# Linear attention and a gated MLP: loading q in 1-KB rows, with the transposed layout and the order of work that follow from it

## The chip, the cores and the metric

The kernel runs on one core of a Trainium2 chip. The metric is the device time of one execution in microseconds (us); medians of several runs are quoted. TensorE does the matmuls, ScalarE and VectorE (ACT and DVE in the profile) copy and combine, GpSimd (POOL) casts and scales, and SyncE (SP) issues most loads. In this kernel matmuls write to PSUM; the tiles that they read lie in SBUF. A run is called slow when it lies over 1.5% above the fastest of its kernel; only fast runs are compared, and a difference counts as faster or slower from 2% on. A profile's span is about 2 us shorter than the time of the same run (156.3 us beside 158.19 us for the profiled run of before).

## The reference

Causal attention with a decay `lam` per head, without softmax, in blocks of 64 tokens with a carried state, feeds a gated MLP whose gate mixes tokens:

```python
# q, k, v: 4 x 8 heads x 768 tokens x 64; lam: 8 heads
for b in range(nb):                                   # blocks of 64 tokens
    intra = einsum('bhic,bhjc->bhij', qb, kb) * Dmask # lam ** (i - j), causal
    out   = intra @ vb + (qb * lam_pow) @ kv_state
    kv_state = lam_block * kv_state + (kb * rev_pow)^T @ vb
x = out as (batch, seq, 512)
h = relu(x @ w_in)                                    # 1024 wide: u, v
v_n = (v - mean(v)) / sqrt(var(v) + 1e-6)
y = (u * (w_spatial @ v_n + b_spatial)) @ w_out
```

## The kernel before

Work is cut into 12 tiles of 256 tokens with all 8 heads, three tiles to a batch. Partition p of a tile holds tokens 2p and 2p + 1 (`m` below), so a packet of a load is 2 tokens x 64 x 4 bytes = 512 bytes. k and q are scaled and cast, transposed on TensorE (tiles 0 to 7), and copied out of PSUM: kT by ScalarE, qT by VectorE, which multiplies the decays in on the way. Scores, a mask and two groups of products build `pat` in PSUM. ScalarE copies it to `xT`, and in doing so puts the tokens, which lie as (m, p), back into the order 2p + m. All projections read `xT`.

```python
def load_x(x, src, n):                    # q, k and v alike: 512-byte rows
    # [...]
    nc.sync.dma_start(out=t.rearrange("p h m d -> p h (m d)"),
        in_=src[b, :, r * T2:(r + 1) * T2].rearrange("h (p m) d -> p h (m d)", m=2))
# [...]
def copy_kT(n):
    nc.scalar.activation(out=transposed(n, "kT"), in_=st[n]["pt"][:, 0], func=AF.Copy)

def copy_qT(n):                           # every tensor bf16 and dense
    nc.vector.tensor_tensor(out=transposed(n, "qT"), in0=st[n]["pt"][:, 1],
        in1=lq[:, n % NR].rearrange("p m g x -> p (m g) x"), op=ALU.mult)
# [...]
def copy_x(n):                            # written at a step of 2 elements
    # [...]
    nc.scalar.activation(
        out=xT[b][:, r].rearrange("p c g (d m) -> p (c g) m d", m=2),
        in_=st[n]["po"].rearrange("p c g (m d) -> p (c g) m d", m=2), func=AF.Copy)
# [...]
order = """
    q:0 q:1 k:0 k:1 v:0 q:2 [...] ld:0 cq:0 q:4 lq:0 cq:1 lq:1 ck:0 k:4
    lq:2 ck:1 k:5 T:0 qT:0 T:1 kT:0 qT:1 cq:2 kT:1 A:0:0 A:0:1 [...]
```

The words of `order` are the program: `q:0` loads q of tile 0, `ck`/`cq` scale or cast, `T` transposes, `A` are the scores, `a` the mask, `xT` the copy above, `pv`/`pu` the projections, `pvs` the token mixing, `po` the output.

## Time and profile before

| | before |
|---|---|
| median time (3 runs) | 158.95 us |
| span of the profiled run | 156.3 us |
| TensorE busy | 132.8 us (85%) |
| VectorE / ScalarE / GpSimd busy | 94.0 / 78.0 / 77.7 us |
| first transposes on TensorE | 11.80 us |
| first v projection | 27.22 us |

Busy time on TensorE alone fills 85% of the span, and most of the rest is the wait at the start. So what a change does to TensorE's holes decides. The prediction below shows the slices, the start of the timeline and the groups. The timeline: start us, duration us, engine, line, operation, out<-in, and in brackets the idle time before and what ended it; PEld is TensorE loading weights.

```profile
25.70 2.48 ACT L308 ACTIVATE xT<-pat 128x1024 bf16<-128x1024 f32 x2 [0.70 <-PE pat L299]
27.22 0.13 PEld L325 LDWEIGHTS <-xT 128*128 128x128 bf16 x2 [0.17 <-ACT xT L308]
27.22 1.99 PE L325 MATMUL pv<-win_sb,xT 128*128 128x512 bf16 x8
```

A copy takes 1.3 us (1322 ns on average), and the projection starts at 27.22 without any hole on TensorE: other matmuls lie between, just long enough to cover the copy. How little room is left shows in the bracket of the weight load: it was already waiting, 0.17 us, for the copy.

### The profile page before, as it was taken

How to read it: one execution, taken by the hardware profiler on the slowest of the kernel's cores; microseconds unless marked ns; L12 is line 12 of the kernel's file. 1: busy time of each engine (PE TensorE's matmuls, PEld its weight loads, DVE VectorE, ACT ScalarE, POOL GpSimd, SP SyncE). 2: the span in 40 equal slices, each digit the busy share in tenths (PEclk: the TensorE clock that was granted, in tenths of full speed). 3: DMA queues.
4: the chain of work that ended last, by engine and by line, in shares of the span. 5: the costliest groups of instructions: out<-in, count | busy, mean ns of one | idle time of the engine just before them, and what ended most of it. 6: DMA issues, size and time to landing. Idle time of an engine off the chain costs nothing.

```text
span 156.3 us, 4534 instructions
## 1 busy us (share of the span) xinstructions
PE 132.8 (85%) x1992; PEld 88.7 (57%) x1992; DVE 94.0 (60%) x167; ACT 78.0 (50%) x103; POOL 77.7 (50%) x63
## 2 busy tenths in 40 slices
PE   0009469989989999989899999999999999999970
PEld 0008469646868667836665567665665557646440
DVE  1401975696967958656982874787395976424510
ACT  3896234564869423546555033658543376022360
POOL 4076966720359299799802059937220066470000
PEclk9999965999999999999999999999999999999996
DMA  2999999999998999994596995991890011006085
GB/s 43 305 291 290 290 247 295 246 261 212 260 271 260 269 277 204 296 292 124 143 294 115 229 244 125 180 268 31 259 256 33 0 72 66 0 0 268 10 319 208
DMA packets 51987, 30.70 MB, mean 196 GB/s; under 512 B 9472, under 2 KB 48896, under 8 KB 51968
## 3 DMA queue, kind: packets, MB, share of 16 engines
q1 hardware_dynamic: 49312, 27.53, 68.3%
q0 software_dynamic: 2368, 2.75, 10.5%
q8 instruction: 15, 0.25, 0.7%
q10 hardware_dynamic: 288, 0.14, 0.3%
q14 instruction: 4, 0.03, 0.1%
HBM read 24.78 MB, written 6.29 MB: 199 GB/s over the span
## 4 chain that ended last, share of the span: by engine, by line
PE 57%; DMA 16%; SPq 9%; ACT 8%; DVE 4%; POOL 3%; issue 1%; POOLq 0%; ACTq 0%
PE pvs L371 20%; PE po L409 12%; DMA k_in<-in_k_dram 11%; PE pv L325 9%; SPq L72 9%; PE pu L360 8%; DMA v_in<-in_v_dram 5%; ACT wt_sb L461 3%; PE pat L299 2%; ACT vh L330 2%; POOL kd L165 2%; PE pt L191 2%; PE pam L227 1%; ACT kT L202 1%; ACT uT L365 1%
## 5 line engine op out<-in xcount | busy, mean ns | idle before, releaser
L235 DVE TENSOR_TENSOR a<-pam,causal 128x1024 bf16<-128x1024 f32 x24 | 28.7, 1219 | 9.2 <-PE pam L227 9.1
L371 PE MATMUL pvs<-wt_sb,vn 128*128 128x384 bf16 x192 | 32.9, 326 | 0.3 <-ACT wt_sb L461 0.2
L397 POOL TENSOR_TENSOR gT<-h,uT 128x768 bf16<-128x768 f32 x12 | 19.6, 1644 | 21.6 <-PE po L409 16.1
L165 POOL TENSOR_TENSOR kd<-k_in,ldec 128x1024 bf16<-128x1024 f32 x12 | 23.3, 1944 | 12.0 <-DMA k_in<-in_k_dram 11.2
L371 PEld LDWEIGHTS <-vn 128*128 128x128 bf16 x192 | 18.4, 98 | 12.3 <-issue 0.2
L360 PE MATMUL pu<-xT,win_sb 128*128 128x256 bf16 x192 | 22.6, 273 | 0.0
L325 PE MATMUL pv<-win_sb,xT 128*128 128x512 bf16 x96 | 22.3, 380 | 0.0
L386 DVE TENSOR_TENSOR h<-pvs,bsp_bc 128x768 f32<-128x768 f32 (+1 forms) x17 | 15.3, 904 | 11.4 <-PE pvs L371 11.4
L431 ACT ACTIVATE o<-po 128x1024 f32<-128x1024 f32 x11 | 11.3, 1023 | 20.5 <-PE po L409 20.1
L337 DVE BATCH_NORM_STATS2 st<-vh 128x6 f32<-128x512 bf16 x24 | 16.1, 672 | 7.9 <-ACT vh L330 7.9
L178 POOL CAST vc<-v_in 128x1024 bf16<-128x1024 f32 x12 | 12.5, 1044 | 16.7 <-DMA v_in<-in_v_dram 16.7
L308 ACT ACTIVATE xT<-pat 128x1024 bf16<-128x1024 f32 x12 | 15.7, 1322 | 9.8 <-PE pat L299 9.8
L360 PEld LDWEIGHTS <-win_sb 128*128 128x128 bf16 x192 | 18.5, 98 | 3.5 <-issue 0.2
L191 PE MATMUL pt<-ident,kd 128*128 128x128 bf16 x64 | 5.8, 242 | 14.2 <-POOL kd L165 14.2
L330 ACT ACTIVATE vh<-pv 128x1024 bf16<-128x1024 f32 x12 | 12.3, 1023 | 10.0 <-PE pv L325 9.2
L409 PE MATMUL po<-wout_sb,gT 128*128 128x512 bf16 x72 | 16.7, 379 | 0.5 <-DVE s L263 0.5
L365 ACT ACTIVATE uT<-pu 128x1024 bf16<-128x1024 f32 x12 | 12.3, 1024 | 8.9 <-PE pu L360 8.9
L325 PEld LDWEIGHTS <-xT 128*128 128x128 bf16 x96 | 9.0, 98 | 10.2 <-issue 0.2
L202 ACT ACTIVATE kT<-pt 128x1024 bf16<-128x1024 bf16 x8 | 8.2, 1022 | 12.8 <-PE pt L191 10.1
L205 DVE TENSOR_TENSOR qT<-pt,lq 128x1024 bf16<-128x1024 bf16 x8 | 5.5, 691 | 14.4 <-PE pt L191 9.7
L352 DVE TENSOR_SCALAR vn<-vh,mv,rstd 128x512 bf16<-128x512 bf16 x24 | 13.3, 596 | 0.4
L191 PEld LDWEIGHTS <-kd 128*128 128x128 bf16 x64 | 4.6, 109 | 15.6 <-POOL kd L165 14.9
(58 smaller groups left out, 154.3 us busy)
## 6 DMA issues: line engine op xcount, KB each, us to landing
q_in<-in_q_dram SPq DMA_DIRECT2D x12, 512.0 KB, 7.5
k_in<-in_k_dram SPq DMA_DIRECT2D x12, 512.0 KB, 7.4
v_in<-in_v_dram SPq DMA_DIRECT2D x12, 512.0 KB, 7.7
out_dram<-o SPq DMA_DIRECT2D x11, 512.0 KB, 2.8
wsp_raw<-in_moe_w_spatial_dram POOLq DMA_DIRECT2D x1, 1152.0 KB, 13.4
win_sb<-in_moe_w_in_dram POOLq DMA_DIRECT2D x2, 512.0 KB, 9.2
...
```

Of the source, the lines that this page charges most:

```text
L72: nc.sync.dma_start(out=t.rearrange("p h m d -> p h (m d)"), in_=src[b, :, r * T2:(r + 1) * T2].rearrange("h (p m) d -> p h (m d)", m=2))
L165: eng.tensor_tensor(out=o, in0=st[n][x], in1=table[:, n % NR].rearrange("p m h -> p h m").unsqueeze(3) .broadcast_to((P, H, 2, D)), op=ALU ...
L235: nc.vector.tensor_tensor(out=s["a"][:, i].rearrange("p h g c x -> p (h g) c x"), in0=s["pam", i].rearrange("p h g c x -> p (h g) c x"), i ...
L308: nc.scalar.activation(out=xT[b][:, r].rearrange("p c g (d m) -> p (c g) m d", m=2), in_=st[n]["po"].rearrange("p c g (m d) -> p (c g) m d ...
L325: nc.tensor.matmul(out=p[:, j], lhsT=xT[b][:, r, j, c, :], rhs=win_sb[:, c, DH:DFF], start=(c == 0), stop=(c == NCH - 1))
L330: nc.scalar.activation(out=vh[:, 2 * r:2 * r + 2, :], in_=ps["v", b, r], func=AF.Relu)
L337: nc.vector.bn_stats(out=st6[:, t, :], in_=vh[:, t, :])
L360: nc.tensor.matmul(out=p[:, f], lhsT=win_sb[:, c, f * P:(f + 1) * P], rhs=xT[b][:, r, :, c, :], start=(c == 0), stop=(c == NCH - 1))
L371: nc.tensor.matmul(out=p[:, i, 0:HW_], lhsT=gm["vn", b][:, s, f * P:(f + 1) * P], rhs=wt_sb[:, s, i * HW_:(i + 1) * HW_], start=(s == 0), ...
L386: nc.vector.tensor_tensor(out=h[:, i], in0=ps["s", b, f][:, i, 0:HW_], in1=bsp_bc.rearrange("p (i x) -> p i x", i=2)[:, i], op=ALU.add)
L397: eng.tensor_tensor(out=gT[:, f, :].rearrange("p (i x) -> p i x", i=2)[:, i], in0=ps["h", b, f][:, i], in1=gm["uT", b][:, f, :].rearrange( ...
L409: nc.tensor.matmul(out=o, lhsT=gT[:, c, t * P:(t + 1) * P], rhs=wout_sb[:, c, f0:f0 + fn], start=(c == 0), stop=(c == NCH - 1))
```

## The change

The intent is cheaper loads of q. A row of q now holds 4 tokens (1 KB); to keep all 128 partitions filled, partition 2p + f holds tokens 4p to 4p + 3 of heads 4f to 4f + 3. Each load becomes two issues, one for each f. What follows from this layout is most of the diff: after the transposes the columns alternate between the two halves of the heads, so copy_qT reads them at a step of two; tokens now lie as (m, p) with m = 4, so copy_x writes at a step of four; the decays of q depend on the partition's parity and need a second small load of `lam`. The order of work was made anew for it.

```diff
+    def load_q(n):
+        b, r = divmod(n, NR)
+        t = st[n]["q"] = fin.tile([P, 4, 4, D], FP32, tag="q", name=f"q_in_{n}")
+        for f in range(2):
+            nc.sync.dma_start(
+                out=t[f::2].rearrange("p j m d -> p j (m d)"),
+                in_=q[b, 4 * f:4 * f + 4, r * T2:(r + 1) * T2].rearrange(
+                    "j (p m) d -> p j (m d)", m=4))
[...]
+    lam_f = const.tile([P, 4], FP32)
+    nc.scalar.dma_start(out=lam_f, in_=lam.rearrange("(f j) -> f j", f=2).unsqueeze(0)
+                        .to_broadcast((D, 2, 4)))
[... tables of positions and decays for the new layout ...]
     def copy_qT(n):
-        nc.vector.tensor_tensor(out=transposed(n, "qT"), in0=st[n]["pt"][:, 1],
-                                in1=lq[:, n % NR].rearrange("p m g x -> p (m g) x"), op=ALU.mult)
+        nc.vector.tensor_tensor(
+            out=transposed(n, "qT").rearrange("p g (f x) -> p g f x", f=2),
+            in0=st[n]["pt"][:, 1].rearrange("p g (x f) -> p g f x", f=2),
+            in1=lq[:, n % NR].rearrange("p m j f x -> p (m j) f x"), op=ALU.mult)
[...]
         nc.scalar.activation(
-            out=xT[b][:, r].rearrange("p c g (d m) -> p (c g) m d", m=2),
-            in_=st[n]["po"].rearrange("p c g (m d) -> p (c g) m d", m=2), func=AF.Copy)
+            out=xT[b][:, r].rearrange("p c g (d m) -> p (c g) m d", m=4),
+            in_=st[n]["po"].rearrange("p c g (m d) -> p (c g) m d", m=4), func=AF.Copy)
[... order: each engine's own words stay in the same order; between two engines the pair qT:1, kT:1 is turned round: ...]
-        lq:2 ck:1 k:5 T:0 qT:0 T:1 kT:0 qT:1 cq:2 kT:1 A:0:0 A:0:1 cv:0 wv v:4 q:5 a:0:0 K:0
+        lq:2 ck:1 k:5 T:0 qT:0 kT:0 T:1 kT:1 qT:1 cq:2 A:0:0 A:0:1 a:0:0 cv:0 wv v:4 q:5 a:0:1
```

More of the change, by code (lines that the diff above doesn't have):

```diff
@@ L44 @@
     NPE = 8
+    CKD = ()
+    CVA = ()
     T2 = 2 * P
@@ L73, in load_x @@
                           in_=src[b, :, r * T2:(r + 1) * T2].rearrange("h (p m) d -> p h (m d)", m=2))
+    def load_q(n):
[6 more added lines that the diff above has]
+                    "j (p m) d -> p j (m d)", m=4))
     lam_bc = const.tile([P, H], FP32)
     nc.scalar.dma_start(out=lam_bc, in_=lam.unsqueeze(0).to_broadcast((P, H)))
+    lam_f = const.tile([P, 4], FP32)
+    nc.scalar.dma_start(out=lam_f, in_=lam.rearrange("(f j) -> f j", f=2).unsqueeze(0)
+                        .to_broadcast((D, 2, 4)))
     kpos_i = const.tile([P, NR, 2], I32)
     nc.gpsimd.iota(kpos_i, pattern=[[-T2, NR], [-1, 2]], base=P - 1, channel_multiplier=-2)
-    qpos_i = const.tile([P, 2, P], I32)
-    nc.gpsimd.iota(qpos_i, pattern=[[1, 2], [2, P]], base=1 - P, channel_multiplier=0)
-    rel_i = const.tile([P, 2, 2, D], I32)
+    qpos_i = const.tile([P, 4, D], I32)
+    nc.gpsimd.iota(qpos_i, pattern=[[1, 4], [4, D]], base=1 - P, channel_multiplier=0)
+    rel_i = const.tile([P, 2, 4, 32], I32)
     for c in range(2):
-        nc.gpsimd.iota(rel_i[c * D:(c + 1) * D], pattern=[[-1, 2], [1, 2], [2, D]], base=0,
+        nc.gpsimd.iota(rel_i[c * D:(c + 1) * D], pattern=[[-1, 2], [1, 4], [4, 32]], base=0,
                        channel_multiplier=-2)
+    tpos_i = const.tile([P, NR, 4], I32)
+    nc.gpsimd.iota(tpos_i, pattern=[[T2, NR], [1, 4]], base=1 - P, channel_multiplier=2)
+    par_i = const.tile([P, 1], I32)
+    nc.gpsimd.iota(par_i, pattern=[[0, 1]], base=0, channel_multiplier=1)
     ident = const.tile([P, P], BF16)
@@ L94 @@
     nc.vector.tensor_copy(out=kpos, in_=kpos_i.rearrange("p r m -> p (r m)"))
-    qpos = const.tile([P, 2, P], FP32)
+    qpos = const.tile([P, 4, D], FP32)
     nc.vector.tensor_copy(out=qpos, in_=qpos_i)
@@ L102 @@
     nc.scalar.activation(out=loglam, in_=lam_bc, func=AF.Ln)
+    loglam_f = const.tile([P, 4], FP32)
+    nc.scalar.activation(out=loglam_f, in_=lam_f, func=AF.Ln)
     kexp = const.tile([P, NBLK, H], FP32)
@@ L116 @@
     ldec = const.tile([P, NR, 2, H], FP32)
-    lq = const.tile([P, NR, 2, NG, P], BF16)
-    lqt = const.tile([P, NR, 2, H], FP32)
+    lq = const.tile([P, NR, 4, 2, 2, D], BF16)
+    par = const.tile([P, 1], FP32)
+    nc.vector.tensor_scalar(out=par_i, in0=par_i, scalar1=1, scalar2=None, op0=ALU.bitwise_and)
+    nc.vector.tensor_copy(out=par, in_=par_i)
+    nc.vector.tensor_scalar(out=par, in0=par, scalar1=-2.0, scalar2=None, op0=ALU.mult)
+    tpos = const.tile([P, NR * 4], FP32)
+    nc.vector.tensor_copy(out=tpos, in_=tpos_i.rearrange("p r m -> p (r m)"))
+    nc.vector.tensor_scalar(out=tpos, in0=tpos, scalar1=par, scalar2=None, op0=ALU.add)
+    texp = const.tile([P, NR * 4, 4], FP32)
+    nc.vector.tensor_tensor(out=texp, in0=tpos.unsqueeze(2).broadcast_to((P, NR * 4, 4)),
+                            in1=loglam_f.unsqueeze(1).broadcast_to((P, NR * 4, 4)), op=ALU.mult)
+    lqt = const.tile([P, NR, 4, 4], FP32)
     sq_t = const.tile([P, 1], FP32)
@@ L126, in query_decays @@
         for g in range(NG):
-            nc.scalar.activation(out=lq[:, r, :, g, :], in_=qpos, func=AF.Exp,
+            f, j = divmod(g, 2)
+            nc.scalar.activation(out=lq[:, r, :, j, f, :], in_=qpos, func=AF.Exp,
                                  scale=logl[:, g:g + 1],
@@ L130, in query_decays @@
         if r == NR - 1:
-            nc.scalar.activation(out=lqt.rearrange("p r m h -> p (r m) h"), in_=kexp, func=AF.Exp,
-                                 scale=-1.0)
+            nc.scalar.activation(out=lqt.rearrange("p r m h -> p (r m) h"), in_=texp, func=AF.Exp)
             nc.scalar.activation(out=sq_t, in_=eps_t, func=AF.Sqrt)
@@ L156, with scaled @@
     xT = {}
-    def cast(n, x, tag, table, eng):
-        t = st[n][tag] = att.tile([P, 2, H, D], BF16, tag=tag, name=f"{tag}_{n}")
+    def scaled(n, x, tag, table, eng, M):
+        t = st[n][tag] = att.tile([P, M, 16 // M, D], BF16, tag=tag, name=f"{tag}_{n}")
         o = t.rearrange("p m h d -> p h m d")
@@ L166, in cast @@
                           in1=table[:, n % NR].rearrange("p m h -> p h m").unsqueeze(3)
-                          .broadcast_to((P, H, 2, D)), op=ALU.mult)
+                          .broadcast_to((P, 16 // M, M, D)), op=ALU.mult)
     def cast_k(n):
-        cast(n, "k", "kd", ldec, nc.gpsimd)
+        scaled(n, "k", "kd", ldec, nc.gpsimd if n not in CKD else nc.vector, 2)
     def cast_q(n):
-        cast(n, "q", "qc", lqt if n >= NPE else None, nc.gpsimd if n else nc.vector)
+        scaled(n, "q", "qc", lqt if n >= NPE else None, nc.gpsimd if n else nc.vector, 4)
     def cast_v(n):
@@ L177, in cast_v @@
         s["vc"] = att.tile([P, H, 2, D], BF16, tag="vc", name=f"vc_{n}")
-        nc.gpsimd.tensor_copy(out=s["vc"], in_=s["v"])
+        if n in CVA:
+            nc.scalar.activation(out=s["vc"], in_=s["v"], func=AF.Copy)
+        else:
+            nc.gpsimd.tensor_copy(out=s["vc"], in_=s["v"])
     def transposed(n, x):
-        t = st[n][x] = att.tile([P, 2, NG, P], BF16, tag=x, bufs=TB, name=f"{x}_{n}")
-        return t.rearrange("p m g x -> p (m g) x")
+        t = st[n][x] = att.tile([P, 8, P], BF16, tag=x, bufs=TB, name=f"{x}_{n}")
+        return t
+    WARM = {}
     def transposes(n):
@@ L187, in transposes @@
         pt = s["pt"] = two_banks([P, 2, 2 * NG, P], f"pt_{n}", BF16)
-        for i, src in enumerate((s["kd"], s["qc"])):
-            for m in range(2):
-                for g in range(NG):
+        for i in range(WARM.get(n, 0)):
+            nc.tensor.transpose(out=pt[:, 0, i % 8, :], in_=ident, identity=ident)
+        for i, (src, M) in enumerate(((s["kd"], 2), (s["qc"], 4))):
+            G = 8 // M
+            for m in range(M):
+                for g in range(G):
                     nc.tensor.transpose(
-                        out=pt[:, i, m * NG + g, :],
+                        out=pt[:, i, m * G + g, :],
                         in_=src[:, m, 2 * g:2 * g + 2, :].rearrange("p h d -> p (h d)"),
@@ L213, in qblk @@
     def qblk(n, g, hh, c):
-        return st[n]["qT"][half(hh), :, g, half(c)]
+        f, j = divmod(g, 2)
+        qT = st[n]["qT"][half(hh)].rearrange("r (m j) x -> r m j x", j=2)[:, :, j]
+        ps_ = slice(c * 32, (c + 1) * 32)
+        if n < NPE:
+            return qT.rearrange("r m (f p) -> r m f p", f=2)[:, :, f, ps_]
+        return qT.rearrange("r m (p f) -> r m p f", f=2)[:, :, ps_, f]
     def scores(n, i):
@@ L227, in scores @@
                         nc.tensor.matmul(out=pam[half(c), hh, g2, m, :],
-                                         lhsT=s["kT"][half(hh), m, g, half(c)],
+                                         lhsT=s["kT"][half(hh), m * NG + g, half(c)],
                                          rhs=qblk(n, g, hh, c), start=True, stop=True)
@@ L462, in copy_wt @@
                              func=AF.Copy)
-    acts = {"k": lambda n: load_x("k", k, n), "q": lambda n: load_x("q", q, n),
+    acts = {"k": lambda n: load_x("k", k, n), "q": load_q,
             "v": lambda n: load_x("v", v, n), "wv": lambda: load_win(1),
@@ L474 @@
     order = """
-        q:0 q:1 k:0 k:1 v:0 q:2 k:2 k:3 v:1 v:2 q:3 v:3 ld:0 cq:0 q:4 lq:0 cq:1 lq:1 ck:0 k:4
-        lq:2 ck:1 k:5 T:0 qT:0 T:1 kT:0 qT:1 cq:2 kT:1 A:0:0 A:0:1 cv:0 wv v:4 q:5 a:0:0 K:0
-        a:0:1 A:1:0 ck:2 k:6 bsp:0 A:1:1 s:0:0 s:0:1 a:1:0 T:2 cv:1 v:5 a:1:1 K:1 kT:2 qT:2 O:0
-        cv:2 v:6 q:6 s:1:0 ai:0 A:2:0 s:1:1 O:1 ck:3 wu k:7 a:2:0 V:0 ai:1 V:1 xT:0 K:2 s:2:0
-        xT:1 A:2:1 a:2:1 pv:0:0 cq:3 ws q:7 T:3 vh:0:0 cv:3 v:7 O:2 qT:3 kT:3 K:3 bn:0:0 cq:4
-        ai:2 A:3:0 V:2 pv:0:1 xT:2 s:3:0 s:3:1 a:3:0 rs:0:0 pv:0:2 vh:0:1 vn:0:0 A:3:1 vh:0:2
-        O:3 a:3:1 pu:0:0 ai:3 bn:0:1 ck:4 k:8 V:3 uT:0:0 pu:0:1 bn:0:2 xT:3 pu:0:2 rs:0:1 uT:0:1
-        vn:0:1 rs:0:2 T:4 uT:0:2 vn:0:2 pv:1:0 kT:4 qT:4 wt:0 vh:1:0 A:4:0 cv:4 v:8 q:8 wt:1
-        a:4:0 wtc:0 wt:2 ck:5 k:9 bn:1:0 wtc:1 pu:1:0 cq:5 q:9 wtc:2 A:4:1 K:4 a:4:1 ck:6 uT:1:0
-        pvs:0:0 s:4:0 rs:1:0 s:4:1 vn:1:0 pvs:0:1 cv:5 h:0:0 T:5 h:0:1 g:0:0 wo pvs:0:2 kT:5
+        q:0 q:1 k:0 k:1 v:0 q:2 k:2 k:3 v:1 v:2 q:3 v:3 ld:0 lq:0 cq:0 q:4 cq:1 lq:1 ck:0 k:4
+        lq:2 ck:1 k:5 T:0 qT:0 kT:0 T:1 kT:1 qT:1 cq:2 A:0:0 A:0:1 a:0:0 cv:0 wv v:4 q:5 a:0:1
+        K:0 A:1:0 A:1:1 ck:2 k:6 bsp:0 s:0:0 s:0:1 a:1:0 T:2 a:1:1 cv:1 v:5 kT:2 qT:2 K:1 O:0
+        cv:2 v:6 q:6 s:1:0 A:2:0 ai:0 s:1:1 O:1 a:2:0 ck:3 wu k:7 V:0 ai:1 V:1 xT:0 K:2 s:2:0
+        xT:1 A:2:1 a:2:1 cq:3 ws q:7 pv:0:0 cv:3 v:7 T:3 vh:0:0 O:2 qT:3 kT:3 cq:4 K:3 bn:0:0
+        ai:2 A:3:0 V:2 pv:0:1 xT:2 s:3:0 s:3:1 a:3:0 rs:0:0 pv:0:2 vh:0:1 vn:0:0 ck:4 k:8 A:3:1
+        vh:0:2 O:3 a:3:1 pu:0:0 ai:3 bn:0:1 V:3 uT:0:0 pu:0:1 bn:0:2 xT:3 pu:0:2 rs:0:1 uT:0:1
+        vn:0:1 rs:0:2 T:4 uT:0:2 vn:0:2 pv:1:0 kT:4 qT:4 wt:0 cv:4 v:8 q:8 vh:1:0 A:4:0 wt:1
+        ck:5 k:9 a:4:0 wtc:0 wt:2 bn:1:0 wtc:1 pu:1:0 cq:5 q:9 wtc:2 ck:6 A:4:1 K:4 a:4:1 uT:1:0
+        pvs:0:0 s:4:0 rs:1:0 s:4:1 cv:5 vn:1:0 pvs:0:1 h:0:0 T:5 h:0:1 g:0:0 wo pvs:0:2 kT:5
         qT:5 cv:6 K:5 h:0:2 O:4 cq:6 A:5:0 ai:4 s:5:0 A:5:1 a:5:0 V:4 g:0:1 pvs:0:3 xT:4 a:5:1
@@ L487 @@
         A:6:1 a:6:0 V:5 pv:1:1 xT:5 a:6:1 cv:7 pv:1:2 vh:1:1 ck:8 bn:1:1 T:7 vh:1:2 cq:8 po:0:0
-        kT:7 qT:7 bn:1:2 rs:1:1 ck:9 pu:1:2 o:0:0 out:0:0 k:10 v:9 dt:8 q:10 vn:1:1 rs:1:2 K:7
-        cq:9 dt:9 v:10 uT:1:2 O:6 s:7:0 A:7:0 ai:6 s:7:1 A:7:1 V:6 a:7:0 cv:8 po:0:1 xT:6 vn:1:2
+        kT:7 qT:7 bn:1:2 rs:1:1 ck:9 pu:1:2 o:0:0 out:0:0 k:10 v:9 dt:8 q:10 vn:1:1 rs:1:2 cq:9
+        dt:9 v:10 K:7 uT:1:2 O:6 s:7:0 A:7:0 ai:6 s:7:1 A:7:1 V:6 a:7:0 cv:8 po:0:1 xT:6 vn:1:2
         pu:2:0 o:0:1 out:0:1 a:7:1 pv:2:0 uT:2:0 cv:9 pvs:1:0 vh:2:0 bn:2:0 pvs:1:1 h:1:0 rs:2:0
```

## The prediction

> **What bounds the kernel now.** I read first the slices of the page, then the chain that ended last, then the order of instructions in the first 25 us, and then the mean durations of the operations that the change touches.
>
> The slices (each 3.9 us; busy tenths, granted clock, DMA):
>
> ```profile
> PE   0009469989989999989899999999999999999970
> DVE  1401975696967958656982874787395976424510
> PEclk9999965999999999999999999999999999999996
> DMA  2999999999998999994596995991890011006085
> ```
>
> TensorE has nothing to do for three slices, is thin until about 23 us, and is then busy in nine tenths of almost every slice to the end. So the sum of matmuls after the start is a floor, and only the start, some 25 us, can be shortened much. DMA is saturated all through that start. DVE has a 9 and a 7 in slices 4 and 5, its densest place before slice 12.
>
> The chain of waits, where it leaves the loads:
>
> ```profile
> 24.39 16.89 DMA k_in<-in_k_dram
> ...
> 41.45 1.94 POOL kd L165
> ...
> 43.43 1.08 PE pt L191 x16
> ```
>
> The chain goes through loads until k of tile 4 lands at 41.28, then kd, the transposes and kT, qT. By this chain a shorter load is worth its whole saving. But TensorE was idle for only 0.47 us before those transposes (the timeline says so), so two chains are nearly level there: the loads, and TensorE's own work, which has run without a hole since 23 us. Hence the view that decides is the timeline of the start:
>
> ```profile
> 11.80 1.04 PE L191 MATMUL pt<-ident,kd 128*128 128x128 bf16 x8 [11.80 <-POOL kd L165]
> 13.79 0.69 DVE L205 TENSOR_TENSOR qT<-pt,lq 128x1024 bf16<-128x1024 bf16 x1 [6.99 <-PE pt L191]
> 14.52 1.02 ACT L202 ACTIVATE kT<-pt 128x1024 bf16<-128x1024 bf16 x1 [1.25 <-DVE qT L205]
> 15.68 0.69 DVE L205 TENSOR_TENSOR qT<-pt,lq 128x1024 bf16<-128x1024 bf16 x1 [1.20 <-PE pt L191]
> 16.29 2.35 DVE L235 TENSOR_TENSOR a<-pam,causal 128x1024 bf16<-128x1024 f32 x2
> 16.41 1.02 ACT L202 ACTIVATE kT<-pt 128x1024 bf16<-128x1024 bf16 x1 [0.87 <-DVE qT L205]
> 19.34 2.35 DVE L235 TENSOR_TENSOR a<-pam,causal 128x1024 bf16<-128x1024 f32 x2
> 22.55 0.69 DVE L205 TENSOR_TENSOR qT<-pt,lq 128x1024 bf16<-128x1024 bf16 x1 [0.86 <-ACT kT L202]
> 23.30 0.64 PE L227 MATMUL pam<-qT,kT 64*64 64x128 bf16 x16 [0.58 <-DVE qT L205]
> ```
>
> Two things are to be seen. The two copies out of one transposed tile never overlap: the second starts 0.03 us after the first ends, and which is second is the order of the program (qT then kT for tiles 0 and 1, kT then qT for tile 2). And DVE runs from 15.7 to 21.7 us with almost no hole. The windows say the same, and give the two DMA rates that I need (columns: busy us of PE, PEld, DVE, ACT, POOL, then clock, DMA share, GB/s):
>
> ```profile
> 10.00:11.00 1.00, 0.00 (x0) 0.00 (x0) 0.00 (x0) 1.00 (x3) 1.00 (x1) 1.00 1.22 291
> 15.00:20.00 5.00, 2.55 (x102) 1.98 (x99) 4.29 (x6) 1.56 (x2) 4.83 (x4) 1.00 1.22 290
> 20.00:25.00 5.00, 4.18 (x112) 3.92 (x114) 4.10 (x6) 1.36 (x3) 3.76 (x3) 0.56 1.20 249
> 152.00:153.00 1.00, 0.00 (x0) 0.00 (x0) 0.00 (x0) 0.00 (x0) 0.00 (x0) 1.00 1.01 379
> ```
>
> The durations, from the groups:
>
> ```profile
> L235 DVE TENSOR_TENSOR a<-pam,causal 128x1024 bf16<-128x1024 f32 x24 | 28.7, 1219 | 9.2 <-PE pam L227 9.1
> L308 ACT ACTIVATE xT<-pat 128x1024 bf16<-128x1024 f32 x12 | 15.7, 1322 | 9.8 <-PE pat L299 9.8
> L330 ACT ACTIVATE vh<-pv 128x1024 bf16<-128x1024 f32 x12 | 12.3, 1023 | 10.0 <-PE pv L325 9.2
> L205 DVE TENSOR_TENSOR qT<-pt,lq 128x1024 bf16<-128x1024 bf16 x8 | 5.5, 691 | 14.4 <-PE pt L191 9.7
> ```
>
> **What the Trainium skill says.** "DMA: Bandwidth & Descriptors", "Why small descriptors are slow (HBM only)", has a fixed cost per packet beside the bytes; the trace agrees, with 291 GB/s in 512-byte rows and 379 in the 2-KB rows of the stores (another direction, so only a guide). "VectorE: DVE Perf Modes", "What auto-detection actually checks", gives the doubled two-source rate only if every tensor is 16-bit with a step of one; the trace agrees, 691 ns for qT (all bf16, dense) against 1219 for the mask (fp32 in), both of 1024 elements. "SBUF — State Buffer", "Door 1: The DMA port swizzle", says in its note on lines of 16 bytes that bf16 may stride by up to 8 elements for free; the trace doesn't quite agree for ScalarE, whose xT (written at a step of 2) takes 1322 ns against 1023 for vh. "TensorE: Matmul & The Clock Gate", "What's actually happening", says that the clock follows recent busy-ness; here it was 0.56 in 20 to 25 us after a hole of 1.93 us.
>
> **The change part by part.**
> Loads of q. Spacing of 512-byte packets is 16 x 512 / 291 = 28.2 ns, of 2-KB packets 16 x 2048 / 379 = 86.5; a line through both gives 47.6 ns for 1 KB, an estimate. A load of q then takes 512 x 47.6 / 16 = 1.52 us instead of 1.80: 0.28 saved. Two lie ahead of k of tile 0 (0.56 us), three ahead of tile 2, five ahead of k of tile 4 (1.4 us). Twice as many issues of q cost nothing: the queue's engine is held back by the transfers.
>
> qT on DVE. It now reads the transposed q at a step of two. It should fall to the single rate, so 1219 ns: +0.53 us, eight times, 4.2 us on DVE, each in series with kT and the scores.
>
> xT on ScalarE writes at a step of 4 instead of 2: I put 0 to 0.3 us on each of 12. Score and inter matmuls read q in shorter runs or at a step of two: 0, by the line note. Setup: some ten small operations and one small load more, perhaps 0.5 us on ScalarE before the first decays, which are wanted only at 13.8 us: 0.
>
> The order. I sorted the words of both orders by engine: all five lists are the same. The words are only interleaved otherwise. What this changes is the serial pair of tile 1, which becomes kT then qT.
>
> Summed along the start: k of tile 0 lands 0.56 earlier, so the transposes begin at 11.24 and those of tile 0 end at 13.1. qT 0 runs to 14.4, kT 0 to 15.5: the scores of tile 0 start as now (15.59), the saving is eaten by qT. Then kT 1 to 16.55 and qT 1 to 17.8 (now 16.37). The masks stand behind qT 1 on DVE: they start at 17.8 instead of 16.4. DVE then has 4 masks and 2 states (4 x 1.22 + 0.83 = 5.7 us), so qT of tile 2 starts at 23.5 and ends at 24.7, where it now ends at 23.24. The scores of tile 2 come 1.4 us late, and TensorE is dense from there: +1.4. qT 3 adds 0.5 (TensorE already waits at that place). The wait for k of tile 4 vanishes: -0.47. qT of tiles 4 to 7 adds 2.1 us of DVE beside dense TensorE work; I let a third through, +0.7. Sum: +2.1, from a profile run of 158.2: about 160.3.
>
> **The rivals.** (1) The loads bind to the end, as the chain says: then -1.4 us at tile 4 and, less one qT, about 158. For it speaks the chain itself; against it the hole of only 0.47 us. (2) The step of two costs DVE nothing: then only the swapped pair costs, about +0.3, with the loads' -0.5 to -1.4 against it: 157.5 to 158.5. Against it the pair 691 and 1219. (3) TensorE's clock: tile 2 follows sooner, the hole shrinks, the clock isn't lowered at 20 us: up to 2 us won, 156.5 to 157. Against it, DVE holds the scores back. (4) xT at a step of 4 costs 0.3 or more and ScalarE, which feeds each v projection, adds 1 to 2 us: 162.
>
> **Range and chances.** My sum says 160.3; rivals 1 to 3 lie 2 to 3 us below it, rival 4 somewhat above, and the change was presumably made to win. I take 159.8, with 157.3 to 162.1. More than 2% faster (under 155.8) needs more than the 1.4 us of the loads: 0.05. More than 2% slower (over 162.1) needs xT or the late qT to come through in full: 0.12.
>
> **What would show it.** Right: qT at about 1220 ns; kT 1 before qT 1; the transposes of tile 0 at about 11.2 us; the scores of tile 2 no earlier than 24 us, after DVE; k of tile 4 landing near 40 us and no wait for it; loads of q at about 345 GB/s. Wrong: qT still near 700 ns, the first v projection (now at 27.2 us) earlier than now, or xT far above 1.3 us.

## The result, and the profile after

The changed kernel takes 168.27 us (median of 4 runs, 168.06 to 168.87), the kernel before 158.54 us beside it (4 runs, 157.47 to 158.96). The ratio is 1.0631, 95% interval 1.0566 to 1.0696: slower, and outside the predicted range. A ratio here is the mean time of one kernel's fast runs over the mean of the other's of the same rounds, so it isn't quite the ratio of the medians quoted. I turn differences of ratios into time with 1% = 1.6 us.

The slices of the page (40 equal parts of the span, busy tenths) no longer show a solid row of nines on TensorE:

```profile
PE   0008568768996999979789998989999989999960
DVE  2502795397978869674990964769685978424410
ACT  3498223957696822777574025767735377022450
```

TensorE's busy time is unchanged (133.0 us beside 132.8), so the 10 us of span are all holes on TensorE. The strided reads that the matmuls now make of qT cost nothing visible.

The page's chain that ended last, by engine and then by line, says who fills the holes. Before, then after:

```profile
PE 57%; DMA 16%; SPq 9%; ACT 8%; DVE 4%; POOL 3%; issue 1%; POOLq 0%; ACTq 0%
PE pvs L371 20%; PE po L409 12%; DMA k_in<-in_k_dram 11%; PE pv L325 9%; SPq L72 9%; PE pu L360 8%; DMA v_in<-in_v_dram 5%; ACT wt_sb L461 3%; PE pat L299 2%; ACT vh L330 2%; POOL kd L165 2%; PE pt L191 2%; PE pam L227 1%; ACT kT L202 1%; ACT uT L365 1%
```

```profile
PE 49%; ACT 22%; DVE 12%; DMA 7%; issue 2%; POOL 2%; SPq 2%; ACTq 0%; POOLq 0%; DVEq 0%
PE pvs L419 16%; ACT xT L356 13%; PE pu L408 9%; PE pv L373 8%; PE po L457 7%; DVE qT L246 4%; DMA k_in<-in_k_dram 4%; DMA v_in<-in_v_dram 3%; PE pt L232 3%; DVE a L283 3%; ACT uT L413 3%; PE pat L347 3%; DVE vn L400 2%; ACT kT L243 2%; PE pam L275 2%
```

The loads have left the chain, 25% (DMA and the SP queue) to 9%; whether because they are cheaper or because something else is now longer, this view can't say. ScalarE has come in with 22% instead of 8%, and the copy `xT`, which wasn't among the lines of before at all, holds 13% of the span. The groups (count | busy us, mean ns | idle before, releaser) give the durations that changed:

```profile
L356 ACT ACTIVATE xT<-pat 128x1024 bf16<-128x1024 f32 x12 | 29.4, 2474 | 9.1 <-PE pat L347 9.1
L246 DVE TENSOR_TENSOR qT<-pt,lq 128x1024 bf16<-128x1024 bf16 x8 | 9.8, 1223 | 14.5 <-PE pt L232 9.2
L373 PE MATMUL pv<-win_sb,xT 128*128 128x512 bf16 x90 | 22.4, 380 | 4.4 <-ACT xT L356 2.6
```

`xT` went from 1322 ns to 2474, 12 times: 13.8 us more of ScalarE. qT went from 691 ns to 1223, as predicted. And the projection `pv`, which before never waited, now stands idle 4.4 us, 2.6 of them put down to the copy. Its line of before:

```profile
L325 PE MATMUL pv<-win_sb,xT 128*128 128x512 bf16 x96 | 22.3, 380 | 0.0
```

Other operations of ScalarE are late as well: the waits of TensorE that the profile puts down to ScalarE add up to 10.1 us (3.4 for `xT`), where before they were 1.5. Nine of the twelve copies lie in the chain of waits (start us, duration us, what); the first and the third of them stand there so:

```profile
26.95 0.88 PE pat L347 x21
27.83 0.02 issue
27.86 2.48 ACT xT L356
30.33 0.05 issue
30.38 0.39 PE pv L373
...
35.96 0.48 PE pat L347 x30
36.44 0.02 issue
36.47 2.46 ACT xT L356
38.92 0.03 ACT rstd L391
38.95 0.03 issue
38.98 1.90 PE pv L373 x8
```

`pat` is finished, the copy begins at once, and TensorE waits for its end. Before, the matmuls in between covered a copy of 1.3 us; they don't cover 2.5.

The start, in the timeline of the changed kernel, shows the other parts:

```profile
12.46 1.03 PE L232 MATMUL pt<-ident,kd 128*128 128x128 bf16 x8 [12.46 <-POOL kd L196]
14.45 1.23 DVE L246 TENSOR_TENSOR qT<-pt,lq 128x1024 bf16<-128x1024 bf16 x1 [6.57 <-PE pt L232]
15.71 1.94 ACT L243 ACTIVATE kT<-pt 128x1024 bf16<-128x1024 bf16 x2 [0.43 <-DVE qT L246]
17.68 1.23 DVE L246 TENSOR_TENSOR qT<-pt,lq 128x1024 bf16<-128x1024 bf16 x1 [2.00 <-ACT kT L243]
18.82 2.35 DVE L283 TENSOR_TENSOR a<-pam,causal 128x1024 bf16<-128x1024 f32 x2
24.18 1.22 DVE L246 TENSOR_TENSOR qT<-pt,lq 128x1024 bf16<-128x1024 bf16 x1
25.45 0.64 PE L275 MATMUL pam<-qT,kT 64*64 64x128 bf16 x16 [1.37 <-DVE qT L246]
```

The transposes of tile 0 begin at 12.46 us, later than before (11.80) and not earlier. The pair of tile 1 is now kT, then qT, so the masks start at 18.82 us instead of 16.29; the scores of tile 2 come at 25.45 us instead of 23.30, after VectorE.

How the delay builds up can be read from where TensorE begins a piece of work in three profiles (one run each; the last column is the first experiment below):

| TensorE begins (us) | before | after | delay | after, with dense xT | delay |
|---|---|---|---|---|---|
| first transposes | 11.80 | 12.46 | 0.7 | 12.60 | 0.8 |
| first v projection | 27.22 | 30.38 | 3.2 | 28.04 | 0.8 |
| first u projection | 36.87 | 41.38 | 4.5 | 38.21 | 1.3 |
| first token mixing | 51.41 | 56.51 | 5.1 | 52.52 | 1.1 |
| last output product | 144.51 | 153.59 | 9.1 | 145.88 | 1.4 |

The loss isn't a delay of the start that is carried along: after the start it grows threefold, over the whole kernel. Part of the difference at the first v projection is TensorE's clock, and not the copy: from 20 to 25 and from 25 to 30 us it was 0.50 and 0.60 in the changed kernel's profile and 0.66 and 1.00 in that with the dense copy, whose `xT` could begin 0.9 us sooner (26.96 instead of 27.86). The whole loss isn't the clock: the four runs of the changed kernel had mean clocks of 0.967, 0.967, 0.992 and 0.997 and took 168.06, 168.29, 168.87 and 168.25 us.

One line of the groups is a false trail. VectorE's normalisation `vn` shows a mean of 818 ns after and 596 before, which looks like 5.3 us of new work. Its median is 414 beside 411 ns; single ones take 2.06 us in one kernel and 2.09 in the other. Only how many of them are long differs, and with the copy dense the mean was 515 ns. So it goes with the copy; whether the long ones cost anything at the end isn't shown.

### The profile page after: what moved, and what is told of

The parts are those of the page before. It is cut to its first block, busy times and chain, and to the rows that moved or that the text cites. A ratio compares the mean times of both kernels' runs of the same rounds, so it can differ in the third digit from the quotient of the medians.

```text
span 166.3 us, 4556 instructions
## 1 busy us (share of the span) xinstructions
PE 133.0 (80%) x1980; PEld 88.5 (53%) x1992; DVE 104.1 (63%) x173; ACT 89.7 (54%) x104; POOL 78.0 (47%) x65
## 4 chain that ended last, share of the span: by engine, by line
PE 49%; ACT 22%; DVE 12%; DMA 7%; issue 2%; POOL 2%; SPq 2%; ACTq 0%; POOLq 0%; DVEq 0%
PE pvs L419 16%; ACT xT L356 13%; PE pu L408 9%; PE pv L373 8%; PE po L457 7%; DVE qT L246 4%; DMA k_in<-in_k_dram 4%; DMA v_in<-in_v_dram 3%; PE pt L232 3%; DVE a L283 3%; ACT uT L413 3%; PE pat L347 3%; DVE vn L400 2%; ACT kT L243 2%; PE pam L275 2%
## 5 line engine op out<-in xcount | busy, mean ns | idle before, releaser
L356 ACT ACTIVATE xT<-pat 128x1024 bf16<-128x1024 f32 x12 | 29.4, 2474 | 9.1 <-PE pat L347 9.1
L400 DVE TENSOR_SCALAR vn<-vh,mv,rstd 128x512 bf16<-128x512 bf16 x24 | 18.6, 818 | 0.4
L246 DVE TENSOR_TENSOR qT<-pt,lq 128x1024 bf16<-128x1024 bf16 x8 | 9.8, 1223 | 14.5 <-PE pt L232 9.2
L275 PE MATMUL pam<-qT,kT 64*64 64x128 bf16 x384 | 11.0, 232 | 8.1 <-ACT seen L334 2.5
L413 ACT ACTIVATE uT<-pu 128x1024 bf16<-128x1024 f32 x12 | 12.3, 1023 | 7.6 <-PE pu L408 7.6
L243 ACT ACTIVATE kT<-pt 128x1024 bf16<-128x1024 bf16 x8 | 8.1, 1024 | 11.4 <-PE pt L232 9.9
```

The costliest lines, as they stand in the source:

```text
L246: nc.vector.tensor_tensor(out=transposed(n, "qT").rearrange("p g (f x) -> p g f x", f=2), in0=st[n]["pt"][:, 1].rearrange("p g (x f) -> p ...
L356: nc.scalar.activation(out=xT[b][:, r].rearrange("p c g (d m) -> p (c g) m d", m=4), in_=st[n]["po"].rearrange("p c g (m d) -> p (c g) m d ...
L400: nc.vector.tensor_scalar(out=vn[:, t, :], in0=gm["vh", b][:, t, :], scalar1=mv[:, t, 0:1], scalar2=rstd[:, t:t + 1], op0=ALU.subtract, op ...
L413: nc.scalar.activation(out=uT[:, :, r * T2:(r + 1) * T2], in_=ps["u", b, r], func=AF.Relu)
```

## The experiments

Thirteen kernels were run. My theory: the copy `xT`, which the prediction had put at 0 to 0.3 us, is nearly the whole loss. Rivals: the slower qT with its place in the serial pair; the order; the start (issues and small loads). For the copy itself there were further rivals on what makes it long: the step of its writes, its number of short rows, the bytes it spreads over, or the engine. Kernels that were run together share a chip and the runs of the kernel before.

### Dense writes of xT in the changed kernel

The step can be moved to the other side: the copy reads PSUM at 32 elements' distance and writes SBUF densely. The result is the same numbers in the same places.

```diff
-            out=xT[b][:, r].rearrange("p c g (d m) -> p (c g) m d", m=4),
-            in_=st[n]["po"].rearrange("p c g (m d) -> p (c g) m d", m=4), func=AF.Copy)
+            out=xT[b][:, r].rearrange("p c g (d m) -> p (c g) d m", m=4),
+            in_=st[n]["po"].rearrange("p c g (m d) -> p (c g) d m", m=4), func=AF.Copy)
```

> The changed kernel, but ScalarE's xT copy reads the four token columns out of PSUM at a step and writes densely, instead of reading densely and writing at a step of 4 (8 bytes). The result stays correct. Theory X (the step-4 write, 2474 ns against 1322, is the main cause, +13.8 us on ScalarE, in series in front of each v projection): xT falls to 1.0 to 1.3 us and the time to 160 to 162 us, that is 6 to 8 of the 9.7 us come back. Theory Q (the 1223-ns qT and the late masks on DVE are the main cause): xT gets shorter but the time stays above 165 us. If the read at a step is itself slow, xT stays above 2 us, and the run says nothing of the total.

Measured: 160.75 us, ratio 1.0133 (1.0069 to 1.0196), correct. Its group, and its timeline at the first projection:

```profile
L356 ACT ACTIVATE xT<-pat 128x1024 bf16<-128x1024 f32 x12 | 12.2, 1022 | 9.2 <-PE pat L347 9.2
```

```profile
26.96 1.94 ACT L356 ACTIVATE xT<-pat 128x1024 bf16<-128x1024 f32 x2 [0.29 <-PE pat L347]
28.04 1.90 PE L373 MATMUL pv<-win_sb,xT 128*128 128x512 bf16 x7
```

The copy falls to 1022 ns, `pv` starts without a hole, TensorE's waits for ScalarE fall to 1.8 us, and 5.0 of the 6.3% come back (1.0631 to 1.0133: 7.9 us). One line of the diff carries most of the loss.

### Dense reads of qT in the changed kernel

The decay table is written interleaved instead, so copy_qT is dense again and the matmuls pick every second column.

```diff
-            nc.scalar.activation(out=lq[:, r, :, j, f, :], in_=qpos, func=AF.Exp,
+            nc.scalar.activation(out=lq[:, r, :, j, :].rearrange("p m (x f) -> p m x f", f=2)[:, :, :, f], in_=qpos, func=AF.Exp,
[...]
-            out=transposed(n, "qT").rearrange("p g (f x) -> p g f x", f=2),
-            in0=st[n]["pt"][:, 1].rearrange("p g (x f) -> p g f x", f=2),
-            in1=lq[:, n % NR].rearrange("p m j f x -> p (m j) f x"), op=ALU.mult)
+            out=transposed(n, "qT"), in0=st[n]["pt"][:, 1],
+            in1=lq[:, n % NR].rearrange("p m j x -> p (m j) x"), op=ALU.mult)
[... and qblk, where the matmuls of tiles 0 to 7 now read every second column ...]
```

> The changed kernel, but qT is copied densely (the even and odd columns are told apart by the matmuls' reads, as the tiles from 8 on do already), so that DVE should be back at about 691 ns. Correct result. Theory X: 8 times 0.53 us less on DVE brings 1.5 to 2.5 us (three of the eight lie in series in the start): 166 to 167 us. Theory Q: 4 us and more, below 164.5. Both expect the matmuls pam and pat at the duration of now (216 ns median).

Measured: 166.48 us with one slow run among four; the fast ones give 1.0452 (1.0362 to 1.0542), correct. qT is back at 690 ns and `xT` stays at 2470. So qT's step is worth 1.8% while the copies are long. It is a part of the loss, but the smaller one.

### The pair of tile 1 put back

```diff
-        lq:2 ck:1 k:5 T:0 qT:0 kT:0 T:1 kT:1 qT:1 cq:2 A:0:0 A:0:1 a:0:0 cv:0 wv v:4 q:5 a:0:1
+        lq:2 ck:1 k:5 T:0 qT:0 kT:0 T:1 qT:1 kT:1 cq:2 A:0:0 A:0:1 a:0:0 cv:0 wv v:4 q:5 a:0:1
```

> The changed kernel with one pair of words exchanged: qT of tile 1 ahead of kT of tile 1, as in the kernel before. Prediction's step (the pair in the wrong order makes the masks of tile 0 start 1.4 us later): the first mask starts at about 17 us instead of 18.82, the time falls by 1.0 to 1.4 us, to about 167. Rival (DVE has slack further on, or the v projection waits for xT and loads anyway): within 0.4 us of 168.3.

Measured: 1.0529 (1.0438 to 1.0619) over three fast runs; the profiled run was a slow one (169.07 us), so its trace is used only for the order of things. There the masks start at 17.63 us instead of 18.82. About 1% comes back, though its interval overlaps that of the changed kernel (1.0566 to 1.0696); the runs "both" and "three" below ask again.

### The step of four alone, in the kernel before

The kernel before with only the two 2s of copy_x made 4s. The tokens then come out in a wrong order, so the result is wrong.

> The kernel before, with only its xT copy changed to write at a step of 4 (as the changed kernel does). Tokens then come out in a wrong order, so the result is wrong on purpose; the work is the same. Theory X: xT takes about 2.47 us and the time goes from 158.5 to 164 to 166 us, that is, 6 to 8 us of the loss come from this alone. Theory Q or a sum of small things: under 162.

Measured: two of four runs slow; the fast ones, 164.76 and 164.33 us, give 1.0357 (1.0281 to 1.0433). The copy in this kernel:

```profile
L308 ACT ACTIVATE xT<-pat 128x1024 bf16<-128x1024 f32 x12 | 29.4, 2472 | 9.1 <-PE pat L299 9.1
```

The step alone makes the copy as long as in the changed kernel, without any of its other parts, and alone costs 5.7 us. This isn't the same step as the 7.9 us above: here the copy grew by 1.15 us, from 1322 ns, there it shrank by 1.45, to 1022, and beside the other parts of the change. How much of the difference is theirs wasn't measured.

### Both, and all three

"Both" joins the dense `xT` and the dense qT; "three" puts the pair of tile 1 back as well. The edits are those above.

> The changed kernel with both repairs: xT written densely (read at a step) and qT copied densely. Correct result. What is left of the change is then the loads of q in 1-KB rows, the two issues for each, the longer setup and the order of tile 1's pair. If the two repairs add up: 160.7 minus some 2 = 158.5 to 159 us, level with before. If the loads in 1-KB rows are worth what the prediction said (1.4 us at tile 4) beyond that, and xT (1.02 instead of 1.32 us) helps too: 157 us or less. If the start (four issues, 0.7 us each, in front of k) costs more than the loads save: 160 and more.

> As the run with both repairs, and also qT ahead of kT for tile 1. The exchange alone moved the first masks from 18.8 to 17.6 us and the mean of the fast runs from 168.3 to 167.3. If the start is on the path that sets the end: 0.5 to 1.2 us less than with both repairs. If the loads bind at tile 4 and swallow it: within 0.3 us.

Measured on one chip: both, 159.99 us, 1.0053 (1.0006 to 1.0101); three, 158.18 us, 0.994 (0.9903 to 0.9976); both correct. Their intervals don't touch: the swapped pair costs 1.1%, 1.8 us, by the ratios. A rival isn't excluded, TensorE's clock: the two profiled runs, both at a mean clock of 0.96, took 159.77 and 159.66 us, and of the other runs those of "three" had 0.970 to 0.998 and those of "both" 0.961 to 0.986. "Both" is also slower than the 158.5 to 159 that was expected if the repairs simply add up. With all three undone nothing slower than before is left, and the kernel is 0.6% faster than before, which is under the 2%.

### Dense writes of xT in the kernel before

The same turn of copy_x with m = 2.

> The kernel before, with xT read at a step out of PSUM and written densely, loads and all else as before. Correct result. xT should take 1.02 us instead of 1.32. If xT lies in series in front of the projections in this kernel too, as it does in the changed one (some 0.5 us of the end for each us of the total, there 13.8 us of ScalarE made about 7 us): 3.6 us of ScalarE make 0.5 to 2 us, 157 to 158. If TensorE is dense whatever xT does: within 0.4 us of 158.6.

Measured: 158.64 us, 0.9982 (0.9951 to 1.0013), correct. The copy fell from 1322 to 1022 ns, 3.6 us of ScalarE in all, and the time didn't move. The copy was already covered by other matmuls. Shortening it is worth nothing where lengthening it costs 5.7 us: the slack was on one side only.

### What makes the copy long

The kernel before, with copies of 128 x 1024 elements out of one PSUM tile appended, each with one property changed (core of the edit):

```diff
+    nc.scalar.activation(out=cols(dst, 2), in_=rows(2), func=AF.Copy)   # 8 groups, write step 2
+    nc.scalar.activation(out=cols(dst, 4), in_=rows(4), func=AF.Copy)   # step 4, as in the changed kernel
+    nc.scalar.activation(out=cols(dst, 8), in_=rows(8), func=AF.Copy)   # step 8
[... one long row at step 2 and at step 4; dense in short rows of 32; reads at step 32, writes dense ...]
[... VectorE: dense, step 2, step 4; ScalarE to fp32: dense, step 2, step 4 ...]
```

> The kernel before with fourteen copies of 128x1024 out of PSUM appended at its end (the outputs don't change, the time of the whole is of no interest): ScalarE to bf16 dense; at steps of 2, 4 and 8 in 8 x step rows; at steps of 2 and 4 as one row; in rows of 32 that are dense inside (32 rows); reading at a step of 32 fp32 and writing densely; VectorE dense and at steps of 2 and 4; ScalarE to fp32 dense, at a step of 2 and at a step of 4. Theory of lines (cost goes by how many 16-byte lines a write touches): dense 1.02, step 2 1.32, step 4 2.47, step 8 more still (about double), one row as many rows. Theory of rows (each row costs): the dense rows of 32 cost as step 4, and the single rows cost 1.02. Theory of bytes (2-byte writes that can't be joined): step 8 as step 4. VectorE: same law if it belongs to SBUF, none if to ScalarE.

It was one look (a single run, so of unknown state; its time means nothing). The timeline of the appended copies, in the order above:

```profile
154.26 1.30 ACT L521 ACTIVATE dst<-mb 128x1024 bf16<-128x1024 f32 x1
155.59 2.43 ACT L522 ACTIVATE dst<-mb 128x1024 bf16<-128x1024 f32 x1
158.05 4.69 ACT L523 ACTIVATE dst<-mb 128x1024 bf16<-128x1024 f32 x1
162.78 1.30 ACT L524 ACTIVATE dst<-mb 128x1024 bf16<-128x1024 f32 x1
164.11 2.43 ACT L525 ACTIVATE dst<-mb 128x1024 bf16<-128x1024 f32 x1
166.58 1.02 ACT L526 ACTIVATE dst<-mb 128x1024 bf16<-128x1024 f32 x1
167.63 1.02 ACT L527 ACTIVATE dst<-mb 128x1024 bf16<-128x1024 f32 x1
...
171.33 2.42 DVE L530 CAST dst<-mb 128x1024 bf16<-128x1024 f32 x1
...
174.90 1.07 ACT L532 ACTIVATE dsf<-mb 128x1024 f32<-128x1024 f32 x1
176.00 1.96 ACT L533 ACTIVATE dsf<-mb 128x1024 f32<-128x1024 f32 x1
```

The first three rows are bf16 at write steps of 2, 4 and 8: 1.30, 2.43, 4.69 us. One long row at the same step (L524, L525) takes just as long, and short dense rows (L526) cost nothing: it isn't the number of rows. Reads at a distance of 32 with dense writes (L527) cost nothing. VectorE pays the same at a step of 4 (L530): it isn't the engine. In fp32 a step of 2 takes 1.07 and a step of 4 takes 1.96 (L532, L533). So the step of the write sets the duration. If one divides by the stretches of 16 bytes that are touched, the bf16 rows give about 4.6 to 5.1 ns each (4.69 us over 1024 of them, 1.30 over 256), but fp32 at a step of 16 bytes touches 1024 too and took 1.96 us, not 4.69. That bf16 pays more than fp32 for the same step in bytes is shown; why is open.

### The step of two in qT alone, and the two issues alone

Two further single parts, put into the kernel before. The first reads qT at a step of two, which mixes up columns and so is wrong. The second loads q in two issues of four heads each, with the old 512-byte rows.

```diff
-        nc.vector.tensor_tensor(out=transposed(n, "qT"), in0=st[n]["pt"][:, 1],
-                                in1=lq[:, n % NR].rearrange("p m g x -> p (m g) x"), op=ALU.mult)
+        nc.vector.tensor_tensor(out=transposed(n, "qT").rearrange("p g (f x) -> p g f x", f=2),
+                                in0=st[n]["pt"][:, 1].rearrange("p g (x f) -> p g f x", f=2),
+                                in1=lq[:, n % NR].rearrange("p m g (f x) -> p (m g) f x", f=2), op=ALU.mult)
```

> The kernel before with only its qT copy changed: it reads the transposed q at a step of two (the decay table is left as it is, so the result is wrong on purpose; the work is that of the changed kernel's copy). qT should take 1.22 us instead of 0.69. Its share of the loss, by itself: the prediction's working gave +0.5 us at three places in the start and a third of 2.1 us later, some 1.5 to 2.2 us: 160 to 161. In the changed kernel the repair was worth 2.3 us (168.3 to 166.0). If only the long xT made it matter: under 159.3.

```diff
[... load_q, as load_x, and its place in the list of words ...]
+        for f in range(2):
+            nc.sync.dma_start(out=t[:, 4 * f:4 * f + 4].rearrange("p h m d -> p h (m d)"),
+                              in_=q[b, 4 * f:4 * f + 4, r * T2:(r + 1) * T2].rearrange(
+                                  "h (p m) d -> p h (m d)", m=2))
```

> The kernel before with each load of q in two issues (heads 0 to 3 and 4 to 7; 512-byte rows and 128 partitions as before). Correct result. In all runs of the changed layout the transfer rate dips to about 90 GB/s at 4 to 5 us, and q of tile 1 lands 0.7 to 0.9 us later than before although its loads are shorter. Theory I (the issues, 0.6 us each, four ahead of k): the dip is here too, the second q is cast after 8.4 us instead of 7.9, the time is 0.3 to 0.8 us longer. Theory L (the second small load, of the decay rates, is what holds the queues): no dip, time as before.

Measured: qT alone 159.92 us, 1.0068 (0.9998 to 1.0137), so about 1.1 us and not quite told from nothing. The issues alone 158.59 us, 0.9991 (0.9926 to 1.0057), correct. In the one profile of that kernel the start is late:

```profile
12.42 1.04 PE L199 MATMUL pt<-ident,kd 128*128 128x128 bf16 x8 [12.42 <-POOL kd L173]
```

That is 0.62 us later than before, and it is gone by the end. That the issues are the cause isn't shown: the start of the kernel with only the step of four is that of before to the letter, and its transposes began at 12.91 us in its profile, while in four profiles with the same loads, that of before among them, they began at 11.76 to 11.83. What is shown is the queue: an issue of q takes SyncE 0.54 us before and 0.68 after, the two ahead of the first k become four, and so that k is issued at 3.51 us instead of 1.87 (2.90 with the issues alone). The issues of q at the start, of the kernel before and of the changed one:

```profile
0.74 1.08 SPq L72 DMA_DIRECT2D q_in<-in_q_dram  x2
```

```profile
0.73 2.73 SPq L82 DMA_DIRECT2D q_in<-in_q_dram  x4
```

### Without the small load, and k ahead of q

Two steps from "three" towards a better kernel. The first drops the second load of `lam` and works its value out on VectorE from the table that is there; the second loads and scales k of tile 0 ahead of q of tile 1.

```diff
-    nc.scalar.dma_start(out=lam_f, in_=lam.rearrange("(f j) -> f j", f=2).unsqueeze(0)
-                        .to_broadcast((D, 2, 4)))
[...]
+    nc.vector.tensor_tensor(out=dlam, in0=loglam[:, 4:8], in1=loglam[:, 0:4], op=ALU.subtract)
+    nc.vector.tensor_scalar(out=dlam, in0=dlam, scalar1=par, scalar2=None, op0=ALU.mult)
+    nc.vector.tensor_tensor(out=loglam_f, in0=dlam, in1=loglam[:, 0:4], op=ALU.add)
```

> As the run with the three repairs (158.2), and without the second load of the decay rates: its four columns are made by three small VectorE operations from the first load. Correct result. Theory L: no dip in the transfer rate at 4 to 5 us, k of tile 0 lands 0.8 us earlier or more (kd at 9.3 to 9.8 us instead of 10.6), and the time falls by 0.3 to 0.8 us. Theory I: the dip stays, kd starts at 10.4 or later, time as with the three repairs; the first key decays come 2 us earlier in either case.

```diff
-        q:0 q:1 k:0 k:1 v:0 q:2 k:2 k:3 v:1 v:2 q:3 v:3 ld:0 lq:0 cq:0 q:4 cq:1 lq:1 ck:0 k:4
+        q:0 k:0 q:1 k:1 v:0 q:2 k:2 k:3 v:1 v:2 q:3 v:3 ld:0 lq:0 cq:0 q:4 ck:0 lq:1 cq:1 k:4
```

> As the run without the second load of the decay rates, and k of tile 0 is loaded ahead of q of tile 1, with its product on GpSimd ahead of the cast of q of tile 1. Correct result. If the first transposes are on the path: they start at 10.6 to 11.2 us instead of 12.5, VectorE's masks end about 1 us earlier, and the time falls by 0.5 to 1 us against the run without that load. If the path in the start is the products and casts of GpSimd for tile 2 (which wait for later loads): within 0.3 us.

Measured: without the load, 157.41 us, 0.9918 (0.9856 to 0.9979); with k first as well, 157.11 us, 0.990 (0.9837 to 0.9962); both correct. Each is faster than the kernel before, by 0.8 and 1.0%, which is under the 2%; the steps from "three" on are too small to be told apart. In the windows (busy us of PE, PEld, DVE, ACT, POOL, then clock, DMA share, GB/s) of 4 to 5 us, the changed kernel and the one without the small load read:

```profile
4.00:5.00 1.00, 0.00 (x0) 0.00 (x0) 0.88 (x8) 0.00 (x0) 0.00 (x0) 1.00 0.39 83
```

```profile
4.00:5.00 1.00, 0.00 (x0) 0.00 (x0) 0.92 (x8) 1.00 (x1) 0.00 (x0) 1.00 0.91 273
```

Before, it was 329 GB/s. All six profiles with this load have the dip (83 to 99 GB/s), the two without it don't (273 and 221), nor has the kernel with the issues alone (279). So this load of a few numbers cut the rate of all loads for about a microsecond, and ScalarE, which is idle in the first row, was waiting for it. Less came of it than expected: without it k of tile 0 is scaled at 10.26 instead of 10.61 us, where 0.8 us or more had been foretold. And with k first the transposes begin at 11.17 instead of 12.25 us, but VectorE's masks don't start sooner (16.92 beside 16.74).

### Are the 1-KB rows worth anything?

The last kernel asks whether the gain of the best version comes from the dense copy and k first, and not from the rows: both put into the kernel before, with the old 512-byte rows (5 rounds).

> The kernel before (512-byte rows of q) with the two things that the last version also has and that are not part of the change: xT written densely, and k of tile 0 loaded and multiplied ahead of q of tile 1. Correct result. The last version, with q in 1-KB rows, is at 0.990 of before. If the 1-KB rows are worth the 1.4 us of the prediction and more: this one stays at 0.997 to 1.000 (as the dense xT alone, 0.998). If the win is the order of the first loads and the rows are worth nothing to the end: 0.990 here too. k of tile 4 should be multiplied from 41 us on (as before) in the first case, against 36.6 us in the last version.

Measured: 158.82 us, 1.0013 (0.9965 to 1.0061), correct. Nothing is gained without the rows; the slowest run of the best version (158.28) is below the fastest of this one (158.35). When k of tile 4 could be scaled, in the timeline of the best version and then of this one:

```profile
36.59 1.93 POOL L196 TENSOR_TENSOR kd<-k_in,ldec 128x1024 bf16<-128x1024 f32 x1 [5.37 <-DMA k_in<-in_k_dram]
```

```profile
41.52 1.93 POOL L165 TENSOR_TENSOR kd<-k_in,ldec 128x1024 bf16<-128x1024 f32 x1 [8.44 <-PE pu L360]
```

With the rows it comes 4.9 us earlier, and 1.1% (1.8 us) of it arrive at the end. The clock isn't the cause here: it was 1.00 from 12 to 35 us in both profiles. This compares the rows together with what comes with them (the decay tables, one load of `lam`, the rest of the order), so the 1.8 us belong to that bundle; in "three", with the rows but with the small load and the old place of k, k of tile 4 was scaled at 40.38 us, 1.1 earlier than before.

## Why the prediction was wrong

The step that failed is the term "xT on ScalarE writes at a step of 4 instead of 2: I put 0 to 0.3 us on each of 12". It measured 1.15 us on each (1322 to 2474 ns), 13.8 us in all. By itself, put into the kernel before, that cost 5.7 us at the end, and making the copy dense in the changed kernel gave 7.9 back. The sum of the prediction had no term for it (1.4 + 0.5 - 0.47 + 0.7), as if the matmuls between would cover it; they didn't. The data for a doubt were on the table: the prediction itself noted that the step of 2 takes 1322 ns against 1023 for the dense copy, which the note about free strides doesn't allow, and still took the next step to cost no more than that first one had. Two points on a curve that already bends are no ground for 0; the duration roughly doubles with each doubling of the step from 2 on.

The mechanism was in rival 4: `xT` feeds each v projection from ScalarE. Its direction was right, its size (0.3 us a copy, 162 us) too small, and it got too little weight.

The other steps, one by one:

- **qT at the single rate, 1219 ns**: right, 1223. Its cost at the end is 1.8% with long copies, 0.8% with short ones (1.0133 to 1.0053), and 0.7% alone; neither of the last two is quite told from nothing.
- **The order**: right. Each engine's own order is unchanged, and only the pair of tile 1 is turned round; the masks were put at 17.8 us and came at 18.82, 1.0 later, with a start that was 1.2 later than foretold. (They start at 16.29 before, not at 16.4 as the text says, and TensorE did have a hole after 23 us: 0.71 us at 31.94.) In "both" against "three" the swap costs 1.8 us by the ratios, with the clock as a rival, where the prediction had 1.4 us for the late scores of tile 2, qT's part in it included.
- **Loads of q**: k of tile 4 was to land 1.4 us earlier; its scaling starts at 39.49 instead of 41.45 us, 1.96 earlier (1.1 to 1.3 in four other fast profiles with these loads), and the transposes after it don't wait, as foretold. The prediction credited 0.5 us at the end; with the three costs undone there is 0.6% (1.0 us) of gain.
- **Twice as many issues cost nothing**: right at the end, as the issues alone show. At the start the first transposes came at 12.46 instead of 11.24 us; how much of that is the issues, which put k 1.6 us later into the queue, stays open.
- **Setup: 0**: wrong in its place. The small load cut the rate of all loads to 83 GB/s for about a microsecond, and k of tile 0 was scaled 0.35 us sooner without it (one profile each). At the end the load is worth some 0.2%, which these runs can't tell from nothing.
- **Matmuls that read in steps: 0**: right, 133.0 us of TensorE beside 132.8.

Taken without `xT`, the sum was +2.1 us; the changed kernel with a dense `xT` is 1.33% slower than before, 2.1 us (dense, and not as before at a step of 2; in the kernel before that made no difference). The agreement is in part luck (qT and the swap 3.1 us instead of 2.6, the loads -1.0 instead of -0.5), but it shows where the 8 us were missed: in one term, and in no other.

The ladder of the whole, each step on the one before:

| kernel | ratio | step |
|---|---|---|
| changed | 1.0631 | |
| xT written dense | 1.0133 | -5.0% |
| and qT dense | 1.0053 | -0.8% |
| and the pair put back | 0.994 | -1.1% |
| and no small load | 0.9918 | -0.2% (not resolved) |
| and k first | 0.990 | -0.2% (not resolved) |

The rungs come from different rounds and chips, each against the kernel before beside it. What stays open is why writes of bf16 at a step cost so much more than those of fp32, how much of the swap's 1.1% is the clock, and how much of the 1.8 us of the last comparison is the rows alone.

## What to carry to other kernels

When a layout makes a load cheaper, follow the permutation to its last copy and ask on which side the step falls: here a read of PSUM in steps was free and a write of SBUF in steps cost 2.4 times the dense copy, so turning one access pattern gave back 7.9 us. Measure the duration of a copy at the new step before trusting a curve through the old one. And a copy that has no wait now may only just be covered: shortening it by 0.3 us gained nothing, lengthening it by 1.15 us cost some 0.5 us each time (5.7 us over 12).

## What the Trainium skill lacked or had wrong

- "SBUF — State Buffer", "Door 1: The DMA port swizzle", gives in its note on lines of 16 bytes 8 bf16 or 4 fp32 elements as the distance that can be strided for free. For writes by ScalarE that isn't so: bf16 at steps of 1, 2, 4, 8 took 1.02, 1.30, 2.43, 4.69 us, and fp32 at steps of 1, 2, 4 took 1.02, 1.07, 1.96. VectorE took 2.42 at a step of 4 in bf16, 1.23 dense.
- The same note says that any non-contiguous pattern in PSUM slows matmuls significantly. It has nothing on copies out of PSUM, where reads by ScalarE at a step of 32 fp32 elements ran at the dense 1.02 us.
- "DMA: Bandwidth & Descriptors", "Anatomy of one DMA — SWDGE (gpsimd) path", breaks down the fixed cost of a DMA for GpSimd's path only. How the time that an issue holds SyncE's queue goes with the shape of the load no page has: q stood there for 0.54 us an issue before (1.08 us for two, all partitions in 512-byte rows) and 0.68 after (2.73 us for four, every second partition in 1-KB rows).
- The same page, "Why small descriptors are slow (HBM only)", speaks of a packet's own cost; that a small broadcast load beside large ones cut the rate of all of them to 83 GB/s for about a microsecond (273 without it) isn't said there.
